# First weights in half-width loads of one K tile, later places in the load queue, and one pool of five PSUM banks, in a fused recurrent-attention and MLP kernel

## The chip, the cores and the metric

One core of one Trainium2 chip. The metric is the device time of one execution in microseconds (us). The kernel before had medians between 189.99 and 191.18 us on several chips, so every kernel was run in turn with the kernel before on the same chip, and ratios are used. Single executions can fall into a slower state at a lower clock.

## The reference, cut to what matters

```python
# attention: B=4, H=8, S=768, D=48, a state per head
for t in range(S):
    cur = einsum('bhd,bhe->bhde', u * k_t, v_t)
    y[:, :, t] = einsum('bhd,bhde->bhe', r_t, state + cur)
    state = w_t[..., None] * state + einsum('bhd,bhe->bhde', k_t, v_t)
x = y.transpose(0, 2, 1, 3).reshape(3072, 384)
h = x @ w_in                      # 384 x 2048
out = maximum(0.01 * h, h) @ w_out    # 2048 x 384
```

The recurrence is done in 24 chunks of 128 time steps: sums of the logarithms of w, exponentials, scaled k and r, their transposes, scores, a mask, y, an update of the state. Each finished y is transposed to be the MLP's input.

## The kernel before: the parts that matter

The kernel plans its own order. Every piece of work is added as a step with an engine, an assumed duration, what it needs and which PSUM pool it takes. A list scheduler then writes one fixed order for each engine. In the profiles below the engines keep to that order, even where the step at the head waits and a later one is ready. One queue gives the order of the loads; they share 12 input buffers.

```python
ps_cum = tc.tile_pool(name="ps_cum", bufs=1, space=PSUM)   # sums
ps_tr  = tc.tile_pool(name="ps_tr",  bufs=1, space=PSUM)   # transposes of k and r
ps_att = tc.tile_pool(name="ps_att", bufs=3, space=PSUM)   # scores, y, state, y transposed
ps_mlp = tc.tile_pool(name="ps_mlp", bufs=3, space=PSUM)   # hidden and output tiles of the MLP

def load_w_in(q):                       # a quarter of the columns, all three K tiles
    t = inpool.tile([128, KT, FQ], F32, name="ws", tag="in")
    nc.sync.dma_start(
        out=t[:], in_=moe_w_in[:, q * FQ : (q + 1) * FQ].rearrange("(t p) n -> p t n", p=128)
    )
    stage["in", q] = t

def cast_w_in(q):
    nc.vector.tensor_copy(out=w_in_b[:, q], in_=stage["in", q][:])
# ... (cut)
def m_copy(q, ts):                      # ScalarE empties an output bank, then issues the store
    osb = osbs[q, ts] = opool.tile([128, NOUT], F32, name="osb")
    nc.scalar.copy(out=osb[:], in_=ops.pop((q, ts))[:])

def m_store(q, ts):
    row = starts[q] + ts * 128
    nc.scalar.dma_start(out=out[row : row + 128, :], in_=osbs.pop((q, ts))[:])
# ... (cut)
queue = [in 0, u, in 1, in 2, w_in 0, in 3, w_in 1, w_in 2, w_in 3, in 4,
         w_out 0..3, in 5, in 6, ...]   # shortened here; "in i" is the four loads of chunk i
```

In the profile hp is a hidden tile (x times w_in), op an output tile, at the scores, trp the transposes of k and r, ws a staged piece of weights, osb an evicted output tile. A K tile is 128 of the 384 rows of w_in; a hidden tile adds up the products of all three.

## Time and profile before

| | before |
|---|---|
| time, median of the three runs given | 190.6 us |
| span of the profiled run | 187.3 us |
| needed matrix work (counts times warm durations) | 160.05 us |
| matrix time lost before the scores of chunk 4 | 20.5 us |
| last quarter of w_out cast | 43.77 us |

The lines behind this are in the prediction. One measure is used all through the document, the **offset** of a chunk: the time at which its scores start, less the needed matrix work that the program puts ahead of them. The needed work uses the prediction's warm durations (an output matmul 162.5 ns, a hidden one 109.2 or 55.8 ns, and so on). The offset is the matrix time lost so far; apart from small errors of the durations it can only grow, and where it jumps the engine waited or ran at half clock.

Busy time of the kernel before by stretch (columns: us, then PE, weight loads, DVE, ACT, POOL busy with the number of instructions, granted clock, DMA share, GB/s):

```profile
18.00:36.00 18.00, 13.94 (x157) 11.03 (x154) 12.55 (x20) 12.02 (x23) 11.60 (x15) 0.91 0.97 250
36.00:60.00 24.00, 23.78 (x281) 17.61 (x278) 16.85 (x26) 12.54 (x27) 13.21 (x15) 1.00 1.06 260
60.00:120.00 60.00, 60.00 (x886) 48.51 (x885) 47.52 (x77) 40.58 (x84) 50.25 (x60) 1.00 1.08 189
```

Of these 102 us the matrix engine loses almost all its idle time before 36 us; after that it is full for 84 us but for 0.2. (Some 1.9 us more are lost between the scores of chunks 15 and 23.)

### The profile page before, as it was taken

The numbers are of one execution on the slowest core, as the hardware profiler recorded it, in microseconds if no ns is written. First come the engines' busy times: TensorE is split into PE (matmuls) and PEld (weight loads), VectorE is DVE, ScalarE is ACT, GpSimd is POOL, SyncE is SP. The second block draws the span as 40 slices with busy tenths as digits, with TensorE's granted clock in tenths as the row PEclk, the third lists the DMA queues.
The fourth block names the chain that finished last, engine by engine and source line by source line (L and its number), as shares of the span: only waits on it lengthen the run. The fifth ranks groups of instructions, "written<-read, shape, count | busy, mean of one in ns | idle before, by whom it ended". The sixth has DMA issues, their size and how long they took to land.

```text
span 187.3 us, 5286 instructions
## 1 busy us (share of the span) xinstructions
PE 177.5 (95%) x2140; PEld 133.0 (71%) x2140; DVE 114.3 (61%) x184; ACT 110.4 (59%) x216; POOL 113.6 (61%) x142
## 2 busy tenths in 40 slices
PE   7999669999999999999999999989999999999993
PEld 2555447866777978787788778768867886787751
DVE  2277895594588799995797667463667575650000
ACT  3465746932756876684785576557455874364721
POOL 3299683804768999999787877464547488420000
PEclk9999978999999999999999999999999999999999
DMA  6999899899999999999999999699999999612012
GB/s 117 197 193 273 190 386 200 273 373 200 238 206 219 228 176 205 200 175 187 179 215 162 188 201 213 128 189 211 196 201 198 138 194 196 173 25 63 0 42 84
DMA packets 125063, 34.80 MB, mean 186 GB/s; under 512 B 118256, under 2 KB 123504, under 8 KB 125040
## 3 DMA queue, kind: packets, MB, share of 16 engines
q1 hardware_dynamic: 121584, 29.76, 83.9%
q10 hardware_dynamic: 3456, 4.72, 7.7%
q8 instruction: 16, 0.26, 0.6%
q14 instruction: 7, 0.06, 0.1%
HBM read 25.36 MB, written 4.72 MB: 161 GB/s over the span
## 4 chain that ended last, share of the span: by engine, by line
PE 74%; SPq 11%; DMA 9%; ACT 2%; issue 2%; DVE 1%; POOL 0%; ACTq 0%; DVEq 0%
PE hp L409 30%; PE op L421 30%; SPq L190 9%; PE at L314 3%; DMA in<-in_r_dram 3%; DMA in<-in_w_dram 3%; DMA ws<-in_moe_w_in_dram 3%; PE cum L234 2%; PE y L339 2%; PE trp L293 2%; PE y L333 1%; PE kv L352 1%; DVE w_in_b L214 1%; PE ytr L380 1%; PE cum L236 1%
## 5 line engine op out<-in xcount | busy, mean ns | idle before, releaser
L409 PE MATMUL hp<-xT,w_in_b 128*128 128x128 bf16 (+1 forms) x912 | 72.5, 235 | 0.7 <-DVE w_in_b L214 0.7
L421 PE MATMUL op<-w_out_b,gt 128*128 128x384 bf16 x384 | 69.7, 326 | 0.0
L409 PEld LDWEIGHTS <-w_in_b 128*128 128x128 bf16 x912 | 62.0, 98 | 6.8 <-DVE w_in_b L214 1.1
L415 ACT ACTIVATE gt<-hp 128x512 bf16<-128x512 f32 x96 | 55.4, 597 | 14.4 <-PE hp L409 11.7
L421 PEld LDWEIGHTS <-gt 128*128 128x128 bf16 x384 | 34.8, 97 | 20.2
L370 POOL TENSOR_TENSOR st<-tt,e 48x192 bf16<-48x192 f32 x40 | 25.9, 648 | 22.5 <-DVE tt L360 19.2
L322 DVE TENSOR_TENSOR mt<-at,tri 128x512 bf16<-128x512 f32 x48 | 30.9, 683 | 11.6 <-PE at L314 11.3
L261 DVE TENSOR_TENSOR kr<-e,in 128x768 bf16<-128x768 f32 x24 | 28.5, 1186 | 11.0 <-ACT e L257 8.3
L265 POOL TENSOR_TENSOR t<-in,ukb 128x384 f32<-128x384 f32 x24 | 26.2, 1090 | 13.2 <-DMA in<-in_r_dram 6.7
L269 POOL TENSOR_TENSOR t<-t,in 128x384 f32<-128x384 f32 x24 | 27.8, 1159 | 5.9 <-DMA in<-in_k_dram 4.8
L284 POOL TENSOR_TENSOR vsc<-in,diag 128x384 f32<-128x384 f32 x24 | 21.3, 887 | 6.9 <-DVE diag L280 4.9
L428 ACT COPY osb<-op 128x384 f32<-128x384 f32 x24 | 11.4, 476 | 23.4 <-PE op L421 23.2
L229 ACT ACTIVATE lw<-in 128x384 bf16<-128x384 f32 x24 | 12.5, 521 | 13.7 <-DMA in<-in_w_dram 13.2
L347 DVE TENSOR_TENSOR ysb<-y,vsc 128x384 bf16<-128x384 f32 x24 | 13.3, 554 | 10.5 <-PE y L339 8.8
L247 DVE SCALAR_TENSOR_TENSOR neg<-cum,lw 128x384 f32<-128x384 f32 x20 | 11.0, 552 | 13.9 <-ACT e L254 13.9
L254 ACT ACTIVATE e<-cum 128x388 f32<-128x388 f32 x24 | 11.9, 495 | 10.5 <-PE cum L236 3.8
L280 DVE TENSOR_REDUCE diag<-t 128x8 f32<-128x384 f32 x24 | 13.1, 544 | 2.8 <-POOL t L269 2.7
L548 PE MATMUL scratch<-idle 128*128 128x512 bf16 x46 | 13.3, 429 | 1.3 <-DVE idle L172 1.3
L276 POOL CAST vb<-in 128x384 bf16<-128x384 f32 x20 | 12.6, 629 | 2.8 <-DMA in<-in_v_dram 2.5
L257 ACT ACTIVATE e<-neg 128x384 f32<-128x384 f32 x20 | 10.5, 524 | 5.6 <-DVE neg L247 5.0
L314 PE MATMUL at<-rkT 48*128 48x128 bf16 x192 | 9.5, 219 | 1.9 <-ACT rkT L298 1.9
L234 PE MATMUL cum<-lw,tri 128*128 128x384 bf16 x24 | 8.0, 335 | 1.9 <-ACT lw L229 1.9
(43 smaller groups left out, 127.8 us busy)
## 6 DMA issues: line engine op xcount, KB each, us to landing
in<-in_w_dram SPq DMA_DIRECT2D x24, 192.0 KB, 4.6
in<-in_r_dram SPq DMA_DIRECT2D x24, 192.0 KB, 4.5
in<-in_k_dram SPq DMA_DIRECT2D x24, 192.0 KB, 4.6
in<-in_v_dram SPq DMA_DIRECT2D x24, 192.0 KB, 4.5
out_dram<-osb ACTq DMA_DIRECT2D x24, 192.0 KB, 3.5
ws<-in_moe_w_in_dram SPq DMA_DIRECT2D x4, 768.0 KB, 6.8
ws<-in_moe_w_out_dram SPq DMA_DIRECT2D x4, 768.0 KB, 7.2
rkT<-kr SPq DMA_TRANSPOSE x13, 4.0
```

Source lines behind the costliest of these rows:

```text
L190: nc.sync.dma_start(out=ins[i][name], in_=src[b, :, c * L : (c + 1) * L, :].rearrange("h p d -> p h d"))
L261: nc.vector.tensor_tensor(out=kr_b[i % NB3][:, :, 0:D], in0=e, in1=ins[i]["kr"], op=ALU.mult)
L265: nc.gpsimd.tensor_tensor(out=t1[:], in0=flat(ins[i]["r"]), in1=ukb[:], op=ALU.mult)
L269: nc.gpsimd.tensor_tensor(out=flat(t2[:]), in0=att[i]["t1"][:], in1=flat(ins[i]["k"]), op=ALU.mult)
L284: nc.gpsimd.tensor_tensor(out=vsc[:], in0=ins[i]["v"], in1=att[i]["diag"][:].unsqueeze(2).to_broadcast([128, H, D]), op=ALU.mult,)
L314: nc.tensor.matmul(ats[x][:, p, :], lhsT=rkT[r0 : r0 + D, 0, p, :], rhs=rkT[r0 : r0 + D, 1, p, :], start=True, stop=True,)
L322: nc.vector.tensor_tensor(out=att[i]["mt"][:, x], in0=att[i]["ats"][x][:], in1=tri[:].unsqueeze(1).to_broadcast([128, NP, 128]), op=ALU.mult,)
L347: nc.vector.tensor_tensor(out=ysb[:], in0=att[i]["y"][:], in1=flat(att[i]["vsc"][:]), op=ALU.add)
L370: nc.gpsimd.tensor_tensor(out=sn[r0 : r0 + D, :, x * D : (x + 1) * D], in0=tt[r0 : r0 + D, :, x * D : (x + 1) * D], in1=el[r0 : r0 + D, :] ...
L409: nc.tensor.matmul(hp[:, jj, :], lhsT=w_in_b[:, wq, t, f0 : f0 + 128], rhs=xT[:, t, t0 : t0 + mb], start=(t == 0), stop=(t == KT - 1),)
L415: nc.scalar.activation(out=gts[q][:, j : j + nj, :], in_=hps.pop((q, j))[:], func=AF.Prelu, alpha=0.01)
L421: nc.tensor.matmul(ops[q, ts][:], lhsT=gts[q][:, j, ts * 128 : (ts + 1) * 128], rhs=w_out_b[:, j, :], start=(j == 0), stop=(j == NFT - 1),)
```

## The change

Its intent: feed the first weights with longer rows (4 KB instead of 2 KB), more of the columns at a time; let the chunk stages share five banks instead of 1 + 1 + 3; use wider MLP blocks and a few more DMA transposes to take work off the matrix engine. The core of the diff (cut: the scheduler's bookkeeping of banks, shifts in the priority of the chunk stages, the place of u's load, other constants):

```diff
-    ps_cum = ...bufs=1   ps_tr = ...bufs=1   ps_att = ...bufs=3
+    ps_att = ctx.enter_context(tc.tile_pool(name="ps_att", bufs=5, space=bass.MemoryType.PSUM))
-    w_in_b = const.tile([128, NQ, KT, FF // NQ], BF16, name="w_in_b")
+    w_in_b = const.tile([128, 2, KT, FF // 2], BF16, name="w_in_b")
     def load_w_in(q):
-        t = inpool.tile([128, KT, FQ], F32, name="ws", tag="in")
-            out=t[:], in_=moe_w_in[:, q * FQ : (q + 1) * FQ].rearrange("(t p) n -> p t n", p=128)
+        half, kt = divmod(q, KT)
+        t = inpool.tile([128, FH], F32, name="ws", tag="in")
+            out=t[:], in_=moe_w_in[kt * 128 : (kt + 1) * 128, half * FH : (half + 1) * FH]
-    sizes = [256, 256, 128 x 13, 256, 128, 256, 256]
+    sizes = [256, 256, 128, 128, 256, 256, 128, 256, 256, 128, 256, 256, 256, 256]
-    BY_DMA = range(11, NCH)   Y_BY_DMA = range(14, NCH)   RCAST = -1  SLACK = 1.2  RACT = 12
+    BY_DMA = range(10, NCH)   Y_BY_DMA = range(12, NCH)   RCAST = 2   SLACK = 0.8  RACT = 8
-    queue = in0 u in1 in2 w_in0 in3 w_in1 w_in2 w_in3 in4 w_out0..3 in5 ...
+    queue = in0 u in1 in2 in3 w_in0 w_in1 w_in2 in4 w_in3 w_in4 w_in5 in5 w_out0..3 in6 ...
-                for _ in range(int((start - at) / 0.22)):                        # warm-up matmuls
+                for _ in range(int((start - at) / (0.45 if at < 4.0 else 0.22))):
```

In the queue the first weights go behind chunk 3, and w_out goes behind chunk 5.

## The prediction

> **What bounds the kernel now.** I read the page first for the busy shares and the DMA queues, then the windows of the first 36 us, then the matrix engine's timeline, then the input queue's issues, and last the end of the chain.
>
> ```profile
> span 187.3 us, 5286 instructions
> PE 177.5 (95%) x2140; PEld 133.0 (71%) x2140; DVE 114.3 (61%) x184; ACT 110.4 (59%) x216; POOL 113.6 (61%) x142
> q1 hardware_dynamic: 121584, 29.76, 83.9%
> q10 hardware_dynamic: 3456, 4.72, 7.7%
> ```
>
> Two resources are nearly full: the matrix engine (95%) and the 16 DMA engines (83.9 + 7.7 = 91.6% of the span, 171.6 us). The other three idle 40%. To see how much of the 177.5 us is needed, I took warm times from dense pieces of the chain: 24 hidden matmuls of 128 columns in 1.34 us (55.8 ns each), 48 of 256 columns in 5.24 us (109.2 ns), four output matmuls in 0.65 us (162.5 ns). Per chunk: scores 0.33, transposes of k and r 0.45, y 0.37, kv 0.17, transpose of y 0.17, sums 0.27 us. Times the counts of the program, the needed work is 160.1 us (hidden 37.5 + 26.2, output 62.4, chunks 34.0). The last matmul ends at 184.1 and the last eviction and store take 3.2 us. So 184.1 - 160.1 = 24.0 us of matrix time are lost. Where?
>
> ```profile
> 20.00:22.00 2.00, 1.20 (x14) 0.97 (x14) 2.00 (x4) 1.60 (x4) 0.83 (x2) 1.00 1.03 192
> 22.00:24.00 2.00, 1.43 (x27) 1.22 (x25) 2.00 (x3) 1.68 (x4) 1.92 (x2) 1.00 0.94 299
> 24.00:26.00 2.00, 1.03 (x19) 0.66 (x16) 1.89 (x4) 1.39 (x2) 1.70 (x3) 0.99 1.04 387
> 26.00:28.00 2.00, 1.67 (x8) 1.19 (x9) 1.86 (x4) 0.17 (x1) 1.47 (x2) 0.50 1.03 384
> 28.00:30.00 2.00, 2.00 (x26) 1.70 (x24) 0.83 (x2) 1.03 (x2) 0.00 (x0) 0.66 1.25 271
> 32.00:34.00 2.00, 2.00 (x22) 1.67 (x21) 0.32 (x1) 2.00 (x5) 1.36 (x2) 1.00 0.47 74
> ...
> 19.93 5.36 DMA ws<-in_moe_w_in_dram
> 25.32 0.97 DVE w_in_b L214
> 26.33 2.74 PE hp L409 x12
> ```
>
> (Windows: stretch, length, PE, weight loads, DVE, ACT, POOL, granted clock, DMA share, GB/s. The last three lines are of the chain.) The engine waits for the first weights. Half idle from 18 to 26, it is put at half clock from 26 to about 29.5, and twelve hidden matmuls take 2.74 us instead of 1.31. From 31.7 us on it is dense: at the scores of chunk 4, at 39.2 us, 18.7 us of work are done, so 20.5 of the 24 lost us lie before. Of the rest, 0.4 lies at 49 us, 0.97 at 125.6 us (a wait for one w load, below) and some 2 in pauses of 0.09 us before most groups of scores.
>
> ```profile
> 120.52 5.46 DMA in<-in_w_dram
> 126.00 0.53 ACT lw L229
> 126.58 0.32 PE cum L234
> ```
>
> The DMA is just as tight. These are w loads on the sync queue, one per chunk (start, duration of the issue):
>
> ```profile
> 49.02 2.34 SPq L190 DMA_DIRECT2D in<-in_w_dram  x1
> ...
> 77.09 0.69 SPq L190 DMA_DIRECT2D in<-in_w_dram  x1
> ...
> 83.91 0.38 SPq L190 DMA_DIRECT2D in<-in_w_dram  x1
> ...
> 150.28 0.77 SPq L190 DMA_DIRECT2D in<-in_w_dram  x1
> ```
>
> Chunks 7 to 13 take (77.09 - 49.02)/6 = 4.68 us each; chunks 14 to 23, with their transposes on the same queue, (150.28 - 83.91)/9 = 7.37 us. A pair of DMA transposes (chunk tile of 256 KB, y tile of 96 KB) costs the stream about 2.7 us, by bytes 2.0 and 0.7 us. The last w lands at 154.2, the scores of the last chunk run at 164.25 right after their transpose (issued 160.14), and y's transpose lands just before the last block starts at 170.8. The end is set by both at once: a full matrix engine, and a stream that delivers just in time.
>
> **What the Trainium skill says.** "TensorE: Matmul & The Clock Gate", Part 1: the clock is halved after an idle window of about 3.4 us and given back after as much activity. The trace agrees: 0.50 and 0.66 in the rows above, after eight half-idle us. The same part gives a fixed 2.5 ns per warm matmul beyond its columns; 55.8 ns for 128 columns and 109.2 for 256 here fit that. "DMA: Bandwidth & Descriptors", Specifications: line rate needs 512 B or more per descriptor. The trace agrees in kind: inputs (rows of 192 B) move at about 197 GB/s, weights in rows of 2 KB at 385. By that page 2 KB is already beyond the knee, so 4 KB should add little. "PSUM — Partial Sum Buffer", Specifications: 8 banks of 2 KiB per partition. The kernel before uses all eight (1 + 1 + 3 + 3), the new one too (5 + 3); no run here shows more.
>
> **The change part by part.**
>
> (a) Less matrix work. The MLP's blocks go from 14 of 128 rows and 5 of 256 to 4 and 10; at 48 hidden matmuls a block they go from 672 narrow + 240 wide to 192 + 480. 480 x 55.8 ns are replaced by 240 x 109.2 ns: 26.8 - 26.2 = 0.6 us less. Chunk 10 moves its k and r transposes to DMA (8 matmuls, 0.45 us), chunks 12 and 13 that of y (2 x 0.17 = 0.33 us). Sum: 1.4 us less, all on a dense engine, so all of it counts if the data are there.
>
> (b) First weights. Before: three chunks, 0.75 MB (a quarter of the columns), chunk 3, the other three quarters. After: four chunks, three loads of 0.5 MB (half of the columns), chunk 4, three more, chunk 5, then w_out. Summing GB/s over the 2 us windows, chunk 2 (2.56 MB with u) is through at about 14.9 us; then chunk 3 at 18.9 (0.79 MB at 197 GB/s = 4.0 us) and the first half at 22.9 (1.57 MB at 388 GB/s = 4.05 us), landing about a us later (before, the bytes of chunk 2 were through at 14.9 and its last cast ran at 16.1), 23.9; the last casts (about 0.66 us each, two thirds of 0.97) bring the first hidden matmul to about 25.2 us instead of 21.2. But then half of the columns is there for two blocks: 48 matmuls, 5.2 us, and 1.9 us of chunk work to do until the second half is cast at about 33 us. With a cold clock (1.4 us lost as before) the engine fills this without a gap. Matrix work done before the first hidden matmul is 6.6 us (before: 5.3), so the loss is 25.2 + 1.4 - 6.6 = 20.0 us, against 20.25 before, counted at 31.7 us. Gain: 0.3 us, give or take 1.5. The later first matmul pays back almost all that the earlier completeness gives.
>
> (c) Casts: 6 x 0.66 instead of 4 x 0.97 us on the vector engine, which idles 40%. Nothing.
>
> (d) Shared banks. A pool of five lets sums and transposes run further ahead. But a dense engine has almost no bank waits to remove: the two pauses of (0.4 + 0.97) us are all, and the second is a load. I give 0.3 us.
>
> (e) More on the DMA: one chunk transpose (2.0 us) and two of y (1.5 us) more, 0.4 less for larger rows (a guess from the nearly flat rate). The holes in the stream around 32 to 34 us (share 0.47, 1 us lost) and 116 to 120 (0.67, 1.3 us lost) may close with fewer, larger weight packets and another order: up to -1.5. Net +1.5 us on the arrival of the last chunk.
>
> Matrix side: -1.4 - 0.3 - 0.3 = -2.0 us, if fed. Stream side: last w at about 155.7 instead of 154.2, at the same 10 us to its scores 165.7; the work after the last scores falls from 19.3 to 18.6 us; so +1.5 - 0.7 = +0.8 us. The later of the two rules, but the ten us of latency can shrink, as part of it was engines working in order (from the w load's landing to the sums 1.5 us, of which the logarithm took 0.52; from the sums to the exponential 1.0 us, behind a state update). I take a point between them nearer to the gain: -1.6 us, **189.0 us**.
>
> **Rivals.**
> 1. *The stream is the bound.* For it: 91.6% DMA, the pace of 7.37 us per chunk against 160.1/24 = 6.7 of matrix work, loads that land just in time, the new order that wants several chunks earlier (chunk 15's scores after 83.4 us of matrix work instead of 87.9). Against: three holes in the stream. Then 190.5 to 192.
> 2. *The start is better than I count.* If the clock stays full through the first hidden matmuls or the halves land 1 to 2 us earlier, 2 to 3 us more are gained: 186 to 187. For it: 4 KB rows need fewer descriptors, so the sync queue stalls less (one input issue took 3.55 us behind a weight load). Against: the engine has even less to do between 18 and 25 us.
> 3. *A stall behind w_out.* It now comes after six chunks; its last quarter lands near 45.2 us (43.4 before), cast at 46.2, where 44 output matmuls begin at about 41. If they run out, 1 us is lost: 190.
>
> **Range and chances.** Between the sides lie 188.6 (all of -2.0) and 191.4 (all of +0.8); with rival 2 the low end is 186.5, and I take 186.5 to 191.6. Faster by 2% means under 186.8: 0.15. Over 194.4: 0.04. Within: 0.81.
>
> **What would show it.** Right: hidden matmuls 672 in all (before 912) and about 1.4 us less needed work; first hidden matmul at 24 to 26 us; a half-clock row near there; dense from then to the end with an offset near 20 us; 14 + 12 DMA transposes. Wrong in (b): a first hidden matmul under 23 us, or clock 1.00 throughout. Wrong in (e): last w landing under 153 us (then nearer 187) or gaps before scores after 100 us (then over 190).

## The result and the profile after

The changed kernel takes 196.12 us in the median (195.35 to 196.44, four runs) against 190.33 (188.53 to 191.79, four runs) before: ratio 1.0331, 95% interval 1.0247 to 1.0415. It is slower. The ratio is the mean time of one kernel's fast runs over that of the other's of the same rounds, so not quite the ratio of the medians.

The page of the kernel after, in the lines that answer to those of before:

```profile
span 193.6 us, 4760 instructions
PE 178.5 (92%) x1881; PEld 128.6 (66%) x1881; DVE 116.0 (60%) x185; ACT 111.3 (57%) x214; POOL 113.6 (59%) x142
q1 hardware_dynamic: 122736, 30.22, 83.0%
```

There is less needed work (158.69 us, 1.36 less), yet 6.3 us more of span. The busy time of PE rose by 1 us all the same, because matmuls at half clock are busy for longer (12 of 256 columns took 2.74 us in the kernel before, 1.31 at full clock): busy time is not work done. The DMA queue's share did not rise, so the stream is no fuller than it was.

Stretches of the kernel after, as above:

```profile
18.00:36.00 18.00, 12.87 (x146) 9.39 (x145) 15.01 (x24) 8.34 (x16) 14.39 (x15) 0.81 1.02 252
36.00:60.00 24.00, 22.61 (x251) 17.01 (x248) 15.56 (x23) 14.23 (x28) 12.57 (x14) 1.00 1.04 260
```

The start is worse (clock 0.81 instead of 0.91, and less of it busy), and 1.2 us more are idle between 36 and 60 us. The offsets say how much:

| offset at the scores of chunk | 3 | 4 | 8 | 23 |
|---|---|---|---|---|
| before | 17.8 | 20.5 | 21.3 | 23.8 |
| after | 17.9 | 24.4 | 27.0 | 31.3 |
| after loses more within the step | 0.1 | 3.8 | 1.8 | 1.8 |

(The last row works with the unrounded offsets.) So 3.9 us go in the start, 1.8 between 39 and 73 us, and 1.8 later; 1.36 come back as less work. That sums to 6.1 of the 6.3 us.

**The start.** Windows of the kernel after:

```profile
20.00:22.00 2.00, 1.05 (x17) 0.64 (x14) 2.00 (x4) 1.84 (x4) 2.00 (x3) 1.00 1.01 215
22.00:24.00 2.00, 1.53 (x29) 1.17 (x30) 1.84 (x4) 1.69 (x3) 1.85 (x3) 1.00 0.83 279
24.00:26.00 2.00, 0.91 (x18) 0.47 (x14) 1.12 (x2) 0.06 (x1) 1.52 (x2) 1.00 1.12 309
26.00:28.00 2.00, 0.37 (x1) 0.10 (x1) 2.00 (x4) 0.52 (x1) 1.74 (x2) 0.51 0.88 162
...
32.00:34.00 2.00, 2.00 (x21) 1.76 (x19) 1.34 (x3) 1.43 (x3) 0.56 (x2) 0.78 0.98 351
```

While the first half of the weights is under way, from 19 to 25 us, the stream never runs at the 388 GB/s that the prediction took. Summed over all windows, chunk 3 is through at 18.95 us, as predicted, and the bytes of one half more at 25.06, where 22.9 was predicted: 6.1 us instead of 4.05. The three loads themselves landed at 22.69, 25.00 and 26.42 us, as packets of chunk 4 came between. The clock is halved from 26.1 us for 6.8 us; in the kernel before it was halved from 26.0 us for 3.4. The chain of work of the kernel after in that place (start, duration, what):

```profile
24.12 1.41 POOL t L271
...
25.56 0.55 DVE diag L282
...
26.49 2.00 DVE w_in_b L216 x2
...
28.54 1.04 PE hp L411 x4
```

The two casts that complete the half stand behind a reduction that waits for GpSimd. Dense hidden work starts at 28.54 us; the prediction had 25.2.

**At 53 to 57 us.** ScalarE of the kernel after (start, duration, engine, line, operation, tiles; in brackets the idle time before and what ended it):

```profile
52.58 0.48 ACT L430 COPY osb<-op 128x384 f32<-128x384 f32 x1 [1.05 <-PE op L423]
53.09 1.31 ACTq L434 DMA_DIRECT2D out_dram<-osb  x1
...
54.90 0.47 ACT L430 COPY osb<-op 128x384 f32<-128x384 f32 x1
```

and its matrix engine there:

```profile
55.42 0.83 PE L411 MATMUL hp<-xT,w_in_b 128*128 128x128 bf16 x12 [0.64 <-ACT osb L430]
56.73 0.44 PE L411 MATMUL hp<-xT,w_in_b 128*128 128x128 bf16 x5 [0.47 <-ACT osb L430]
```

The first store's issue holds ScalarE for 1.31 us (the median of this kernel's 24 stores is 0.34). The eviction behind it is late, and hidden matmuls wait for an eviction (`<-ACT osb`): no bank of the MLP's three is free. In the kernel before the same first store was:

```profile
46.85 0.37 ACTq L432 DMA_DIRECT2D out_dram<-osb  x1
```

**Late.** One hidden group waits 0.98 us at 152 us for a transpose of y by DMA, one group of scores 0.63 us at 128 us for one of k and r. The last w load is issued at 156.59 us instead of 150.28.

### The profile page after: what moved, and what is told of

Its sections match the earlier page's. It is cut to its first block, busy times and chain, and to the rows that moved or that the text cites.

```text
span 193.6 us, 4760 instructions
## 1 busy us (share of the span) xinstructions
PE 178.5 (92%) x1881; PEld 128.6 (66%) x1881; DVE 116.0 (60%) x185; ACT 111.3 (57%) x214; POOL 113.6 (59%) x142
## 4 chain that ended last, share of the span: by engine, by line
PE 70%; POOL 8%; DMA 7%; DVE 5%; issue 4%; ACT 2%; ACTq 1%; SPq 1%; POOLq 0%; DVEq 0%
PE hp L411 27%; PE op L423 27%; DMA in<-in_w_dram 4%; PE at L316 3%; DMA xT<-ysb 3%; PE scratch L553 3%; POOL vsc L286 2%; POOL st L372 2%; PE cum L236 2%; PE trp L295 2%; PE y L341 2%; POOL t L271 2%; POOL t L267 2%; PE y L335 1%; DVE kr L263 1%
## 5 line engine op out<-in xcount | busy, mean ns | idle before, releaser
L411 PE MATMUL hp<-xT,w_in_b 128*128 128x256 bf16 (+1 forms) x672 | 74.2, 260 | 5.3 <-DVE w_in_b L216 3.1
L417 ACT ACTIVATE gt<-hp 128x512 bf16<-128x512 f32 x96 | 56.5, 597 | 27.8 <-PE hp L411 25.0
L411 PEld LDWEIGHTS <-w_in_b 128*128 128x128 bf16 x672 | 56.5, 98 | 14.9 <-DVE w_in_b L216 3.9
L423 PEld LDWEIGHTS <-gt 128*128 128x128 bf16 x384 | 35.7, 98 | 19.6
L267 POOL TENSOR_TENSOR t<-in,ukb 128x384 f32<-128x384 f32 x24 | 26.1, 1090 | 23.5 <-DMA in<-in_r_dram 16.2
L372 POOL TENSOR_TENSOR st<-tt,e 48x192 bf16<-48x192 f32 x40 | 26.7, 667 | 16.4 <-DVE tt L362 13.4
L263 DVE TENSOR_TENSOR kr<-e,in 128x768 bf16<-128x768 f32 x24 | 29.2, 1215 | 9.8 <-DMA in<-in_k_dram 5.4
L286 POOL TENSOR_TENSOR vsc<-in,diag 128x384 f32<-128x384 f32 x24 | 22.5, 937 | 14.5 <-DVE diag L282 7.5
L271 POOL TENSOR_TENSOR t<-t,in 128x384 f32<-128x384 f32 x24 | 27.0, 1125 | 2.8 <-DMA in<-in_k_dram 1.5
L278 POOL CAST vb<-in 128x384 bf16<-128x384 f32 x20 | 11.7, 585 | 0.9 <-DMA in<-in_v_dram 0.7
L362 DVE TENSOR_TENSOR tt<-kv,st 128x384 f32<-128x384 f32 x16 | 8.8, 549 | 1.9 <-PE kv L354 1.5
```

Source lines behind the costliest of these rows:

```text
L263: nc.vector.tensor_tensor(out=kr_b[i % NB3][:, :, 0:D], in0=e, in1=ins[i]["kr"], op=ALU.mult)
L267: nc.gpsimd.tensor_tensor(out=t1[:], in0=flat(ins[i]["r"]), in1=ukb[:], op=ALU.mult)
L271: nc.gpsimd.tensor_tensor(out=flat(t2[:]), in0=att[i]["t1"][:], in1=flat(ins[i]["k"]), op=ALU.mult)
L286: nc.gpsimd.tensor_tensor(out=vsc[:], in0=ins[i]["v"], in1=att[i]["diag"][:].unsqueeze(2).to_broadcast([128, H, D]), op=ALU.mult,)
L372: nc.gpsimd.tensor_tensor(out=sn[r0 : r0 + D, :, x * D : (x + 1) * D], in0=tt[r0 : r0 + D, :, x * D : (x + 1) * D], in1=el[r0 : r0 + D, :] ...
L411: nc.tensor.matmul(hp[:, jj, :], lhsT=w_in_b[:, wq, t, f0 : f0 + 128], rhs=xT[:, t, t0 : t0 + mb], start=(t == 0), stop=(t == KT - 1),)
```

## The experiments

All 18 kernels gave the reference's result. The names say which kernel was edited: a_ is an edit of the kernel after, b_ of the kernel before. Offsets are left out for the three whose profile fell in the slow state (a_warm, a_oldw, a_rows2k). Each offset is of one profiled execution. Kernels with the same program up to chunk 4 differ there by up to 1.1 us (b_wout_late 22.1, b_late_store 21.0; after 24.4, a_wout 24.2, a_store 24.9), so a difference of 1 us between two offsets is not read as an effect.

| run | ratio to before | 95% interval | offset at chunk 4 | at 8 | at 23 |
|---|---|---|---|---|---|
| after | 1.0331 | 1.0247 to 1.0415 | 24.4 | 27.0 | 31.3 |
| a_warm | 1.0360 | 1.0258 to 1.0462 | | | |
| b_cold | 1.0043 | 0.9948 to 1.0138 | 21.3 | 22.9 | 24.7 |
| a_cast | 1.0326 | 1.0248 to 1.0405 | 23.5 | 29.0 | 33.4 |
| a_warm_cast | 1.0310 | 1.0221 to 1.0399 | 23.4 | 27.9 | 31.9 |
| a_oldw | 1.0074 | 1.0018 to 1.0129 | | | |
| b_neww | 1.0285 | 1.0196 to 1.0374 | 25.8 | 29.5 | 32.1 |
| b_psum | 0.9988 | 0.9955 to 1.0021 | 21.0 | 22.0 | 25.1 |
| a_rows2k | 1.0196 | 1.0100 to 1.0292 | | | |
| b_order | 1.0190 | 1.0106 to 1.0274 | 23.2 | 26.8 | 28.4 |
| b_ktiles | 1.0181 | 1.0110 to 1.0252 | 24.6 | 25.0 | 29.3 |
| a_onedma | 1.0241 | 1.0160 to 1.0322 | 25.5 | 28.3 | 31.5 |
| b_psum_sizes | 1.0040 | 0.9989 to 1.0090 | 20.4 | 22.0 | 25.6 |
| a_cols | 1.0290 | 1.0220 to 1.0359 | 25.6 | 28.3 | 30.6 |
| a_wout | 1.0108 | 1.0043 to 1.0173 | 24.2 | 25.0 | 27.3 |
| a_fix | 1.0268 | 1.0187 to 1.0348 | 25.6 | 26.5 | 30.3 |
| b_wout_late | 1.0244 | 1.0144 to 1.0344 | 22.1 | 27.7 | 29.8 |
| b_late_store | 1.0213 | 1.0122 to 1.0304 | 21.0 | 25.0 | 27.6 |
| a_store | 1.0195 | 1.0136 to 1.0254 | 24.9 | 26.7 | 30.0 |

### First round: is it the warm-up or the casts?

Suspects at the start: the changed kernel runs fewer warm-up matmuls at the very start, its casts of the first half stand late in the vector engine's order, and its loads land late. a_warm gives the kernel after the old number of warm-up matmuls; b_cold gives the kernel before the new number:

```diff
-                for _ in range(int((start - at) / (0.45 if at < 4.0 else 0.22))):   # a_warm; b_cold is the reverse
+                for _ in range(int((start - at) / 0.22)):
```

a_cast moves the second and third cast ahead of the reduction of chunk 3 in the written order, and a_warm_cast does both:

```diff
+    at3 = [n for n, x in enumerate(rest) if x[0][0] is a_diag and x[0][1][0] == 3][0]
+    pairs = rest[:at3] + casts + rest[at3:]
```

> The changed kernel with the old count of warm-up matmuls ahead of the first sums (nine again instead of four). Theory 1, a cold clock: the ten warm-up matmuls after the first sums take 2.3 us instead of 4.2, the scores of chunk 0 come at about 9.7 us instead of 11.05, and as every link after it in the chain of waits up to the weight casts is compute, most of that carries to the end: 1.0 to 2.0 us faster than the changed kernel, 194 to 195 us, ratio to before about 1.02 to 1.025. Theory 2, the weights come too late (half of the columns needs 1.5 MB): the casts wait for the transfers, scores of chunk 0 earlier but the second hidden matmul still near 27.6 us and the time within 0.5 us of 196.

> The kernel before with the new, smaller count of warm-up matmuls ahead of the first sums. Theory 1: the ten after the first sums run cold in 4.2 us, scores of chunk 0 at about 11 us instead of 9.7, and the kernel loses up to 1.3 us (ratio 1.004 to 1.010), less if the old order has room there since its first hidden matmuls wait for weights at 19.6 us. Rival: no effect (ratio within 0.003) since the start is bound by the input stream.

> The changed kernel with the second and third weight casts moved ahead of two small operations of chunks 3 and 2 (a reduction and a state sum) in the vector engine's order; nothing else moves. Theory 3, the casts are held in the queue by work that itself waits for GpSimd: casts at 24.7 to 26.7 instead of 26.5 to 28.5, dense hidden matmuls from 26.7 instead of 28.5, 1 to 2 us faster than the changed kernel (194 to 195 us). Theory 2: the casts start no earlier than 26 us as they wait for the transfers, no change.

> Both: warm-up as before and casts ahead. If theories 1 and 3 hold and add, 2 to 3 us faster than the changed kernel (193 to 194 us). If they are the same two us seen from two sides, as good as the better one of the two alone. Theory 2: no change.

Measured: 1.0360, 1.0043, 1.0326 and 1.0310. Neither suspect is the cause: putting the old warm-up back gains nothing, and taking it from the kernel before costs nothing that shows. With the casts moved ahead they wait for the loads instead. The vector engine of a_cast:

```profile
25.78 0.88 DVE L216 CAST w_in_b<-ws 128x1024 bf16<-128x1024 f32 x1 [0.52 <-DMA ws<-in_moe_w_in_dram]
27.15 0.69 DVE L216 CAST w_in_b<-ws 128x1024 bf16<-128x1024 f32 x1 [0.49 <-DMA ws<-in_moe_w_in_dram]
```

The last third of the half lands at 27.1 us in this run, 3.2 later than the prediction's 23.9. Dense hidden work then starts at 27.90 instead of 28.54 us. So the cast order is a second limit close behind the loads: in the kernel after itself the last third landed at 26.42 us and was cast from 27.49. a_cast's offset at chunk 4 is 0.9 us lower than that of the kernel after, within the noise; between chunks 4 and 8 its profile then loses 5.5 us where the kernel after loses 2.6, at the stop that the later rounds are about (its first store's issue took 2.50 us).

### Second round: which part of the change is it?

a_oldw undoes the weight part in the kernel after (quarters, rows of 2 KB, the old queue, the old assumed durations). b_neww is the kernel before with the weight part alone. b_psum is the kernel before with the five shared banks alone. a_rows2k keeps everything of the kernel after but pads the staged tile so that each load moves rows of 2 KB:

```diff
-        t = inpool.tile([128, FH], F32, name="ws", tag="in")                      # a_rows2k
-            out=t[:], in_=moe_w_in[kt * 128 : (kt + 1) * 128, half * FH : (half + 1) * FH]
+        t = inpool.tile([128, 2, FH // 2 + 8], F32, name="ws", tag="in")
+            out=t[:, :, 0 : FH // 2],
+            in_=moe_w_in[kt * 128 : (kt + 1) * 128, half * FH : (half + 1) * FH].rearrange("p (a n) -> p a n", a=2),
```
```diff
-    ps_cum = ...bufs=1   ps_tr = ...bufs=1   ps_att = ...bufs=3                    # b_psum
+    ps_att = ...bufs=5   (cum and trp take their banks from it, the scheduler likewise)
```

> The changed kernel with the weight part undone: quarters of the columns in rows of 2 KB, the old order of loads and the old casts; the five shared banks, the wide blocks, the scheduler's constants and the extra DMA transposes stay. Theory W, the weight loads cost the start: the offset of the scores of chunk 4 (start time less matrix work done before) falls from 24.4 back to about 20.5 to 21.5 us, and the time by 3 us or more, to 191 to 193 us (ratio 1.00 to 1.015). Theory S, the reordered schedule (banks, ranks, wide blocks) costs it: offset at chunk 4 may fall, but stalls after 50 us stay, and the ratio stays above 1.02.

> The kernel before with the weight part alone (halves of the columns one K tile at a time in rows of 4 KB, the new order of loads and the smaller casts); old banks, blocks, constants. Theory W: the offset at chunk 4 rises from 20.5 to about 24 us, ratio 1.015 to 1.025. Theory S: within 1% of before.

> The kernel before with the five shared PSUM banks alone (the scheduler's account of free banks with it). Theory W: within 1% of before (the matrix engine of before waits for no bank). Theory S, if the shared banks let one chunk hold up another: ratio over 1.01.

> The changed kernel with the six weight loads cut into rows of 2 KB (a padded buffer keeps the two halves of a row apart); the same bytes in the same order, and casts of the same size. If rows of 4 KB themselves are slower (mean packet 220 ns against 2 x 95 ns for 2 KB), the third load lands 0.5 to 1 us earlier than 27.1 us and up to 1 us is gained (195 to 196 us). If the amount that must land first is what matters, no change: within 0.5 us of 196, third cast again near 27 us.

Measured: 1.0074, 1.0285, 0.9988, 1.0196. The weight part (form, place in the queue, and with it w_out's later place) alone makes the loss, and undone it takes most of it away. Five shared banks neither gain nor cost (the interval holds 1.0 within 0.5%). Rows of 2 KB do not raise the time, and the interval overlaps that of the kernel after, so no effect of the row length is shown in either direction. The sign that was set for "no change", a third cast near 27 us, came: 27.36, in a profile of the slow state. What remains of the change without its weight part was predicted to gain and does not (1.0074).

### Third round: the form of the loads, their place in the queue, the wide blocks

b_order keeps the quarters of the kernel before and uses the new places. b_ktiles uses the new loads at the old places. a_onedma loads each half in the kernel after by one DMA that takes the three K tiles of each row block together; its halves get buffers of their own, and the input pool shrinks from 12 to 10 buffers (so too in a_cols and a_fix below), which was not tested apart. b_psum_sizes adds the wide blocks to b_psum.

```diff
-    queue = in0 u in1 in2 w_in0 in3 w_in1 w_in2 w_in3 in4 w_out0..3 in5 ...
+    queue = in0 u in1 in2 in3 w_in0 w_in1 in4 w_in2 w_in3 in5 w_out0..3 in6 ...     # b_order
+    queue = in0 u in1 in2 w_in0 in3 w_in1 ... w_in5 in4 w_out0..3 in5 ...            # b_ktiles
```
```diff
+            t = stage["half", half] = const.tile([128, KT, FH], F32, name=f"wst{half}")   # a_onedma
+                out=t[:], in_=moe_w_in[:, half * FH : (half + 1) * FH].rearrange("(t p) n -> p t n", p=128)
```

> The kernel before with the new place of the weights in the input queue alone: its four quarter loads stay (512 columns of all three K tiles, rows of 2 KB), but two come after chunk 3, two after chunk 4, and w_out after chunk 5. Theory O, the later place in the queue costs the start: offset of the scores of chunk 4 at 23 to 24 us instead of 20.5, ratio 1.015 to 1.02. Theory P, the slow transfer of single K tiles costs it: offset 21 to 22 us, ratio under 1.01, since two quarters move at 360 GB/s.

> The kernel before with the new form of the weight loads alone (half of the columns, one K tile at a time, rows of 4 KB, six casts) at the old place in the queue (one load before chunk 3, five after it, then chunk 4 and w_out). Theory P: 4 KB packets again near 290 ns for the first two of the five, the loads take about 2 us longer than the quarters, and since the first hidden matmul needs three loads it comes at about 25 us instead of 21; ratio 1.01 to 1.02. Theory O: ratio under 1.005.

> The changed kernel with each half of the columns loaded by one DMA of 1.5 MB that takes the three K tiles of a partition one after the other, still in rows of 4 KB, at the same place in the queue; same casts. If loading one K tile at a time is what makes the transfer slow, the packets take 160 to 190 ns in the mean instead of 220, the half moves in 4 to 4.5 us instead of 5.5, lands at 25 to 26 us, and 1 to 1.5 us are gained (ratio 1.025). If rows of 4 KB or any burst of weights is slow, packets again 220 ns and no gain.

> A search for a better version: the kernel before with the five shared banks and the wider blocks, with its old weights, constants and queue. Matrix work falls by 0.6 us (480 narrow matmuls become 240 wide); the start should stay as before (offset 20.5 to 21 at chunk 4). Ratio 0.99 to 1.0; over 1.01 if blocks of 256 make the last chunks of a block wait for each other's transposes.

Measured: 1.0190, 1.0181, 1.0241, 1.0040. Place and form each cost about as much and do not add up to more than 1.0285. But b_order also has w_out behind chunk 5, which alone costs 1.0244 (fifth round), so its 1.0190 does not say what the place of the first weights costs in time; its offset at chunk 4 is 2.7 us above before's. b_ktiles says where the form costs: its offset is already 24.6 at chunk 4, though its first load is in its old place. Of three loads that must be there before a hidden tile can be finished, two come behind chunk 3. And a_onedma shows that the transfer itself can be faster. Its windows and its vector engine:

```profile
20.00:22.00 2.00, 1.44 (x18) 0.90 (x17) 2.00 (x5) 1.16 (x3) 2.00 (x2) 1.00 0.99 372
22.00:24.00 2.00, 1.30 (x21) 0.89 (x22) 1.85 (x3) 1.68 (x4) 1.85 (x4) 1.00 1.03 370
```
```profile
24.77 0.69 DVE L217 CAST w_in_b<-wst 128x1024 bf16<-128x1024 f32 x1 [0.37 <-DMA wst<-in_moe_w_in_dram]
26.35 0.55 DVE L283 TENSOR_REDUCE diag<-t 128x8 f32<-128x384 f32 x1 [0.88 <-POOL t L272]
...
27.28 1.98 DVE L217 CAST w_in_b<-wst 128x1024 bf16<-128x1024 f32 x2
```

372 and 370 GB/s where the kernel after had 215 and 279: the whole half is there at 24.77 us. But two of its casts now sit behind the reduction, and the offset at chunk 4 is no better (25.5). Its ratio met the expectation (1.025), but with that offset not for the reason expected, and its interval overlaps that of the kernel after. So a_cast and a_onedma each take one of two limits away and meet the other; neither gains more at the start than the noise. Both together were not run.

At this point the loss after 38 us had no cause. Half of it looked as if it belonged to w_out.

### Fourth round: w_out's place, and attempts at a repair

a_cols is a_onedma with four DMAs of 256 columns for each half. a_wout moves w_out ahead of chunk 5 in the kernel after, and nothing else. a_fix is a_onedma with the first half ahead of chunk 3, the second ahead of chunk 4 and w_out ahead of chunk 5.

```diff
-    queue = ... in4 w_in3 w_in4 w_in5 in5 w_out0..3 in6 ...
+    queue = ... in4 w_in3 w_in4 w_in5 w_out0..3 in5 in6 ...                       # a_wout
+    queue = in0 u in1 in2 w_in0..2 in3 w_in3..5 in4 w_out0..3 in5 ...             # a_fix
```

> Kernel after, each half of the first weights loaded by four DMAs of 256 columns, the three K tiles interleaved in each (rows of 1 KB, 8 DMAs in all instead of 6), everything else as in after. Theory K (a load of a single K tile is slow at its start, where interleaved K tiles are not): as with one DMA per half, first half moved in 5.4 us from first to last packet instead of 7.1, ratio to before 1.020 to 1.026 (after: 1.033). Theory N (what counts is how many DMAs and how long their rows are, not which addresses follow one another): no faster than after or slower, 1.033 to 1.040, transfer 7 us or more. The late place stays in both, so none of them reaches 1.01.

> Kernel after with the four w_out loads put ahead of chunk 5 in the queue; loads of the first weights as in after. Theory W (the stop of 1.5 to 1.9 us at 54 to 57 us comes from the last quarter of w_out being cast at 50.08 us, so that several output tiles end at once and their evictions hold the hidden banks): the last cast at 46 to 48 us, the offset between chunk 8 and the start of chunk 7's rows no longer jumps at 54 to 57 us, 1.5 us or more gained, ratio 1.020 to 1.027. Rival P (the order of the steps and the eviction engine alone): the stop stays or moves, ratio 1.030 to 1.036. Chunk 5 comes later in both, which can cost up to 1 us.

> Attempt at a repair of after: each half by one DMA with the K tiles interleaved, first half ahead of chunk 3, second half ahead of chunk 4, w_out ahead of chunk 5. Theory Q (place in the queue and form of the load make the whole loss): dense hidden work from about 25 to 26 us, offset at chunk 4 of 20.5 to 22 us, ratio 1.000 to 1.012. Rival R (half of the columns at once is by itself worse than quarters, as 1.57 MB must land before anything runs): offset still over 23, ratio 1.015 to 1.025. A gain over before (under 0.99) is expected by none.

Measured: 1.0290, 1.0108, 1.0268.

**a_wout** won back far more than expected. Its stretches and its first store:

```profile
18.00:36.00 18.00, 12.74 (x147) 9.37 (x146) 15.01 (x24) 8.52 (x17) 14.27 (x16) 0.81 0.99 256
36.00:60.00 24.00, 24.00 (x258) 18.29 (x257) 15.24 (x22) 15.22 (x30) 12.04 (x13) 1.00 1.10 257
```
```profile
48.56 0.37 ACTq L434 DMA_DIRECT2D out_dram<-osb  x1
```

The start is as bad as in the kernel after (clock 0.81, 12.74 us busy). From 36 us the engine never stops: 24.00 of 24, and the issue takes 0.37 us again. From chunk 4 to 23 the offset grows by 3.1 us, where before it grew by 3.3 and after by 6.9. So nearly all that the kernel after loses beyond its start goes away when w_out comes one chunk earlier. Of these 3.8 us, 1.8 lie between chunks 4 and 8. The other 2.0 come later and are not clearly w_out's: from chunk 8 to 23 the kernel after grows by 4.3, but a_cols, with w_out late too, by 2.3 as a_wout does.

**a_cols** speaks for theory N on the transfer. Its half took 7.2 us from first to last packet (7.3 in the kernel after, 5.6 in a_onedma), and its first cast waited for its load until 26.52 us, where a_onedma's waited until 24.77. So taking the K tiles together is not enough to make the transfer quick. Its ratio lies between the two expectations.

**a_fix** missed. Its half was cast by 23.9 us, but chunk 3 now came late (scores at 32.58 us), the clock had dropped by then, and hidden work began at 26.8 us, when the transposed input was ready. Earlier weights took their time from the chunk that the hidden work also needs. Neither expectation had that mechanism; the numbers (offset 25.6, ratio 1.0268) are close to rival R's.

### Fifth round: w_out's place alone, in the kernel before

```diff
-    queue = ... in4 w_out0..3 in5 ...
+    queue = ... in4 in5 w_out0..3 in6 ...       # b_wout_late: kernel before, nothing else
```

> Kernel before with one edit: chunk 5 ahead of the four w_out loads in the queue, as in after; first weights, banks, blocks and everything else as before. Theory W (the late place of w_out costs what a_wout won back, about 3 to 4 us, whatever the first weights look like): offset unchanged at chunk 4 (about 20.5), 1.5 us or more above before's by chunk 15, ratio 1.012 to 1.022. Rival S (the late place only hurts where the start has already put everything late, as before's matrix engine has the hidden work of narrow blocks to fill with): offset within 0.7 us of before's at every chunk, ratio 0.998 to 1.006.

Measured: 1.0244. One swap in the queue makes the kernel before about 4.6 us slower, which is above both expectations. The offset grows by 5.6 us from chunk 4 to 8, where it grew by 0.75 before. (Its 22.1 at chunk 4 goes with a clock that dropped twice, at 21.5 and 28.4 us, instead of once at 26 us, with the same queue up to there; b_late_store has 21.0.) ScalarE and the matrix engine of b_wout_late:

```profile
51.59 0.48 ACT L428 COPY osb<-op 128x384 f32<-128x384 f32 x1 [1.06 <-PE op L421]
52.10 3.09 ACTq L432 DMA_DIRECT2D out_dram<-osb  x1
55.23 0.48 ACT L388 COPY xT<-ytr 128x384 bf16<-128x384 bf16 x1 [3.16 <-issue]
```
```profile
56.14 0.83 PE L409 MATMUL hp<-xT,w_in_b 128*128 128x128 bf16 x12 [2.19 <-ACT osb L428]
```

The same picture as in the kernel after, only larger. It also holds in every kept trace, the two store runs aside: with w_out behind chunk 5 the first store's issue takes 0.87 us (a_cols) to 3.09 (b_wout_late), with w_out ahead of it 0.37 to 0.45. The growth from chunk 4 to 8 divides the table in the same way: 1.7 us at most with w_out ahead (before, b_cold, b_psum, b_psum_sizes, b_ktiles, a_wout, a_fix), 2.6 or more with w_out behind (after, a_cast, a_warm_cast, b_neww, b_order, a_onedma, a_cols, b_wout_late), the two store runs aside and the slow profiles left out.

### Sixth round: is it the slow issue?

Both kernels with the stop got one edit, the first block's two stores issued by GpSimd:

```diff
-        nc.scalar.dma_start(out=out[row : row + 128, :], in_=osbs.pop((q, ts))[:])
+        eng = nc.gpsimd if q == 0 else nc.scalar
+        eng.dma_start(out=out[row : row + 128, :], in_=osbs.pop((q, ts))[:])
```

> The kernel b_wout_late (before with chunk 5 ahead of w_out) with one more edit: the first block's two stores are issued by GpSimd instead of ScalarE. In b_wout_late the first store's issue held ScalarE for 3.09 us at 52.1 us, and the evictions behind it came late. Theory E (that issue makes the stop): the 2.19 us wait of the hidden matmuls at 56 us falls under 0.5 us, offset at chunk 6 of 25.5 or less instead of 27.49, ratio 1.008 to 1.016. Rival B (the stop is made by output tiles that all end at once and by data of chunk 6 that comes late, the slow issue only fills the wait): offset at chunk 6 still over 26.5, ratio 1.020 to 1.027.

> The kernel after with the first block's two stores issued by GpSimd instead of ScalarE. There the first store's issue held ScalarE for 1.31 us. Theory E: the waits of 0.64 and 0.47 us before hidden matmuls at 55 to 57 us go, 1 us gained, ratio 1.024 to 1.029. Rival B: no gain, 1.030 to 1.036.

Measured: 1.0213 and 1.0195. The stop itself goes. GpSimd of b_late_store issues the store in 0.72 us, and the matrix engine's longest wait at that place is 0.22 us instead of 2.19 (the earlier line is read below):

```profile
52.28 0.72 POOL L433 DMA_DIRECT2D out_dram<-osb  x1 [0.62 <-ACT osb L428]
```
```profile
43.55 0.82 PE L421 MATMUL op<-w_out_b,gt 128*128 128x384 bf16 x4 [1.00 <-DVE w_out_b L217]
...
55.47 0.83 PE L409 MATMUL hp<-xT,w_in_b 128*128 128x128 bf16 x12 [0.22 <-ACT gt L415]
```

The offset at chunk 6 is 24.8 instead of 27.5, as theory E had it. The ratio is not: 1.0213 lies in the rival's range (its interval reaches into theory E's), and the growth from chunk 4 to 8 is still 4.0 us, against 0.75 before. a_store gained more than expected, but its 1.0195 and the 1.0331 of the kernel after come from different chips, and their intervals still touch.

So the slow issue is a real part of the cost, but not all of it. Between chunks 5 and 6, where the stop is, the growth falls from 3.8 to 1.2 us in b_late_store and from 2.0 to 0.8 in a_store. Over chunks 4 to 8 that leaves only 1.6 and 0.8 us, because the growth from chunk 4 to 5, before any store, came out 1.0 and 0.5 us larger in these two profiles. The trace of b_late_store shows much of the rest: 2.7 of its 4.0 us lie between chunks 4 and 5, where the matrix engine waits 1.00 us for the first cast of w_out (at 43.55 us) and 0.40 and 0.34 us for chunk 4's mask and chunk 5's scaled k and r. Output matmuls could start at 39.57 us in the kernel before. No run took this part away alone.

## Why the prediction was wrong

It gave 189.0 us, 186.5 to 191.6, and 0.81 to "within 2%". It came out at 196.12 us, in the range over 194.4 that it had given 0.04. By its own steps:

- **(a) Less matrix work, -1.4 us: right as a count, not as a gain.** 672 hidden matmuls and 158.69 us of needed work are there. But the two kernels with wide blocks and the old weights did not get it: b_psum_sizes (0.6 us less work, which would be 0.997) is at 1.0040, a_oldw (1.4 us less, 0.993) at 1.0074. The sentence "all on a dense engine, so all of it counts if the data are there" failed in its condition. The trace of b_psum_sizes shows where: between 67 and 70 us the matrix engine waits 0.16, 0.79 and 1.03 us for y, for the transposed k and r and for the logarithm of one chunk each, where neither before nor b_psum has a pause over 0.15 us between 66 and 82 us. That the wide blocks cause these pauses was not tested.
- **(b) First weights, a gain of 0.3 us: the first of two steps that failed.** "the first half at 22.9 (1.57 MB at 388 GB/s = 4.05 us)" measured 6.1 us. The rate was taken from the middle of a transfer of 2.36 MB in another form, and the prediction's own fence showed 299 GB/s in the two us in which that transfer began. The size alone does not make it slow: a_onedma moved the same bytes while the stream ran at 372 and 370 GB/s. The landing then came at 26.4 instead of 23.9 us (27.1 in a_cast), two casts of 1.0 instead of 0.66 us stood behind GpSimd's work, and dense work began at 28.54 instead of 25.2: 3.3 us. The half clock lasted 6.8 instead of 3.4 us, about 2.0 us lost where 1.4 was taken over from before, and one wait of 0.5 us at 34.7 us followed. 20.0 + 3.3 + 0.6 + 0.5 is the 24.4 measured. The sign "first hidden matmul at 24 to 26 us" came true by the letter only: one ran at 24.73, on the first K tile, and the next waited 2.61 us. The prediction also took the trace to agree with the Trainium skill's idle window of about 3.4 us; the last section says what the trace shows.
- **(c) Casts, "nothing": wrong as a reason, right in size.** The vector engine idles 40%, but in its fixed order the two casts that mattered stood behind a reduction. Moving them (a_cast) gained 0.6 us at the first dense matmul, where the loads were the next limit, and nothing in the time, as the stop behind w_out came out larger in its profile.
- **(d) Shared banks, 0.3 us: not contradicted.** b_psum measured 0.9988, and its interval holds a gain of 0.3 us and none at all.
- **(e) More on the DMA, +1.5 us on the last chunk: not the cause.** The last w was issued 6.3 us later, because everything was later. In a_wout, with the same DMA work, it was issued at 152.16 us, 1.9 after before. The gaps after 100 us that were to show (e) wrong did come, and cost 1.8 us more than before; a_wout has the same transposes and does not have that loss. What made these gaps larger in the kernel after was not shown.
- **Rival 3, "a stall behind w_out", 1 us: the right place with the wrong size, and the second step that failed, as the sum left it out.** It expected the last cast at 46.2 us and output matmuls that run dry. The cast ran at 50.08. What stopped in the kernel after was mainly something else: output tiles ended later, the first store's issue held ScalarE, and evictions freed no bank. Output matmuls that waited for w_out's first cast were seen too, in other kernels (1.00 us in b_late_store, 0.57 in a_cast). Moving w_out back (a_wout) takes 3.8 us out of what the offset gains after chunk 4; moving it alone (b_wout_late) costs about 4.6 us of time.
- **Rival 2 said "4 KB rows need fewer descriptors, so the sync queue stalls less".** The issue behind the first half took 4.52 us, against 3.55 before. The other way round.

In short: about half of the loss is a late start, about half is gone when w_out stands ahead of chunk 5, and less work gave 1.4 us back. What stays open: why several loads of a half started more slowly than one large load; what stretches the store's issue; whether the wide blocks make the pauses that eat their gain. No version beat the kernel before; b_psum equals it.

## What to carry to other kernels

Where loads are consumed as they land, a late swap in the load queue can cost more than the saving in the work (here about 4.6 us against 1.4): check both the load that moved back and the one that now waits behind it, even if the latter lands only a few us later. Do not take a stream's steady rate for a shorter piece in another form (here 388 GB/s were taken and 257 came). And where engines run in a fixed order, removing one of two limits that lie 1 us apart shows little: look for the second before calling the first innocent.

## What the Trainium skill lacked or had wrong

- "Perfetto Trace Analysis", DMA Optimizations, advises larger transfers and names the step from 2 KB to 4 KB or 8 KB as one that "can dramatically improve throughput". Read as the length of a row, which is what this change did, it did not: the first half's bytes moved at 257 GB/s on average (1.57 MB in 6.1 us) in rows of 4 KB, and the kernel with rows cut back to 2 KB was not slower (1.0196 against 1.0331, intervals overlapping). The next item of that list, smaller pieces let some work start sooner, is the one that this case supports: at chunk 4 the offset is 20.5 us with quarters (before) and 24.6 with halves (b_ktiles) at the old place in the queue, 23.2 (b_order) and 25.8 (b_neww) at the new one.
- "DMA: Bandwidth & Descriptors", Specifications, has a size for line rate, a ceiling and a first-byte latency, but nothing on a transfer that stays slow for its first 4 us: windows of 215, 279 and 309 GB/s for three loads of one K tile, 372 and 370 for one DMA of the same bytes.
- No page says how far the issue of one and the same store can stretch: by ScalarE it took from 0.34 us to 3.09 here, 192 KB each time, with every activation behind it waiting. "Perfetto Trace Analysis", What "DMA-bound" means, says that the window of an issue is the making of descriptors and not the movement of data; the same page, under "DMA Instruction — HWDGE", counts a wait for the lock of a generator that sequencers share into that window. Whether such a wait stretched it was not tested: SyncE was issuing loads during the slow issues, but during the quick one of the kernel before as well.
- "TensorE: Matmul & The Clock Gate", Part 1, gives an idle window of about 3.4 us as what halves the clock, and does not say how idle the window has to be. In the kernel before the clock was halved at 26.0 us though no pause of the matrix engine since 18 us was over 0.97 us. The length of the window fits: the half clock lasted 3.4 us there, 6.8 in the kernel after and 10.2 in b_neww.
